# Moving one more block to transposed output, narrowing the key-value sums by two columns, and feeding the idle products from a constant

## The chip, the cores and the metric

The kernel runs on one core of one Trainium2 chip. The metric is device time in microseconds of that core for one execution; lower is better. Six executions of the kernel before lie within 0.7 us of each other (266.28 to 266.99). The granted TensorE clock was 1.0. The engines are called TensorE (PE in the profile; PEld is its weight load), DVE (vector), ScalarE (ACT), POOL and SP, which here only issues transfers.

## The reference, cut to what matters

```python
xn = layernorm(x)                                  # x: 2048 tokens x 640
q, k, v = split(xn @ wqkv)                         # 32 heads of 20
phi_q, phi_k = concat(softmax(+p), softmax(-p))    # p = q @ w_phi, k @ w_phi
kv = phi_k^T v ;  z = sum over tokens of phi_k     # per head, 40 x 20 and 40
o = (phi_q kv) / (phi_q z + 1e-6)
out = x + o @ wo + (silu(xn @ w1) * (xn @ w3)) @ w2     # hidden width 1536
```

Linear attention and a gated MLP share the normalised input. Their two output products are added to the residual `x`.

Of the kernel before, what the change touches and what calls it, by code (L numbers as in the profile page):

```python
# [3 lines left out]
ACT = mybir.ActivationFunctionType  # L4
ALU = mybir.AluOpType
# [4 lines left out]
D = 640  # L10
H = 32
# [234 lines left out]
def bass_parallel_sum__linear_kernel_hedgehog__glu_gated_swiglu__prompt_kernel(  # L246
# [14 lines left out]
    LEAD = 5  # L261
    AHEAD = 0
    PACE = 2.6
    f32 = DT.float32
    P = _Program(nc)

# [49 lines left out]
    WVK = new("WVK", [128, DC, 2 * D], bf, RKV)  # L316
    EqT0 = new("EqT0", [128, QC, 512], bf, RKV)
    xT2 = new("xT2", [128, DC, 512], bf, RKV)
    xT = {1: xT1, 2: xT2}

    RH = region(24576)
    hT0 = new("hT0", [128, FC, 512], bf, RH)
# [5 lines left out]
    w2_s = new("w2_s", [128, FC, D], bf, RE + 12288)  # L328
    EqT1 = new("EqT1", [128, QC, 512], bf, RE + 27648)
    hT = [hT0, hT1, hT2, hT3]  # L330
    ot = {1: new("ot1", [128, 4, D], bf, RH + 12288), 2: new("ot2", [128, 4, D], bf, RX)}

    RV = region(21504)
    v2 = new("v2", [128, T, H * 21], bf, RV)
    oT = new("oT", [128, DC, S], bf, RV)

    RW = region(13696)
# [57 lines left out]
    def memset(eng, o, v):  # L395
        P.op(eng, "memset", [o], [], (o, v), cost=0.15 + free(o) / 960)
# [52 lines left out]
    def consts_late():  # L449
        memset("POOL", FM[:], 1.0)  # L450
        select(FM[:], 0, [[0, 6], [-2 * DH, 3]], 1, ALU.is_ge, 0.0)
        select(FM[:], 2 * DH, [[0, 6], [2 * DH, 3]], -1, ALU.is_gt, 0.0)
        memset("POOL", v2[:].rearrange("p t (h c) -> p t h c", c=21)[:, :, :, DH], 1.0)


    def ln_sums(t, q):
# [39 lines left out]
    def ln_apply(t, lo=0, hi=D):  # L496
# [4 lines left out]
        else:  # L501
            P.op("ACT", "activation", [o], [o, s, z], (o, o, ACT.Identity), dict(bias=z, scale=s),
                 cost=0.9)

    def keep_warm(n, rep, rate=2400):
        for _ in range(rep):
            mm(bank(7, 128 * n), zero[:], zero[:].unsqueeze(1).to_broadcast([128, n, 128]), True, True,
               cost=128 * n / rate)

    def warm_up():  # L510
        keep_warm(4, 8, 1200)
        keep_warm(1, 9, 1200)

    def xn_transpose(t, k, c0=0, c1=DC):
        for dc in range(c0, c1):
# [30 lines left out]
        evac(dst.rearrange("p (b c) -> p b c", c=320), bank2(k, 320))  # L546


    def v_out(t, q, k):
        o = v2[:, t, 336 * q:336 * q + 336].rearrange("p (h c) -> p h c", c=21)[:, :, 0:DH]  # L550
        i = bank(k, 320).rearrange("p (h c) -> p h c", c=DH)
        if t < 2 or t == 2 and q == 0:
            copy("ACT", o, i)
        else:
            evac(o, i)

    def v_half(t, q, lo, hi):
        if lo == 0:
            held[t, q] = banks(1)
        k = held[t, q]  # L560
        for i in range(lo, hi):
            mm(bank(k, 320), xnT[:, i, t * 128:(t + 1) * 128], WVK[:, i, 320 * q:320 * q + 320],
               i == 0, i == DC - 1)
        if hi == DC:
            v_out(t, q, held.pop((t, q)))

    def v_first(lo, hi):
        if lo == 0:
            for q in range(2):
                held[0, q] = 2 + q  # L570
        for i in range(lo, hi):
            for q in range(2):
                mm(bank(2 + q, 320), xnT[:, i, 0:128], WVK[:, i, 320 * q:320 * q + 320], i == 0, i == DC - 1)
        if hi == DC:
            for q in range(2):
                v_out(0, q, held.pop((0, q)))
# [14 lines left out]
    def vk_features(t, k):  # L591
        for q, lo, hi in ((0, 0, 512), (1, 512, 1024), (2, 1024, 2 * D)):
            for i in range(DC):
                mm(bank(k + q, hi - lo), xnT[:, i, t * 128:(t + 1) * 128], WVK[:, i, lo:hi], i == 0, i == DC - 1)
        act(v2[:, t, :].rearrange("p (h c) -> p h c", c=21)[:, :, 0:DH],
            PS[:, 512 * k:512 * k + D].rearrange("p (h c) -> p h c", c=DH), ACT.Copy)
        k_exps(t, 512 * k + D)

    def q_features(t, k):
# [39 lines left out]
    def kv_sum(half, k):  # L639
        c0, c1 = ((0, 6), (6, QC))[half]  # L640
        for c in range(c0, c1):
            n = min(63, H * 21 - 63 * c)
            for t in range(T):
                m = min(128, (T - t) * 1280 - 120 * c)
                f = ekt[:].rearrange("p t f -> p (t f)")[:, 1280 * t + 120 * c:1280 * t + 120 * c + m]
                mm(bank(k, n, 63 * (c - c0))[0:m, :], f, v2[:, t, 63 * c:63 * c + n],
                   t == 0, t == T - 1, True, 0.03)
        w = c1 - c0 - half
        for a, b, g in ((0, w, 3), (w, c1 - c0, 2))[0:1 + half]:
            o = KVc[:, c0 + a:c0 + b, 0:21 * g].rearrange("p c (g d) -> p c g d", d=21)  # L650
            i = bank(k, 21 * g * (b - a), 63 * a).rearrange("p (c g d) -> p c g d", g=g, d=21)
            m = FM[:, a:b, 0:g]
            tt("DVE", o[:, :, :, 0:DH], i[:, :, :, 0:DH], m.unsqueeze(3).to_broadcast([128, b - a, g, DH]), ALU.mult)
            stt(o[:, :, :, DH], i[:, :, :, DH], DEN_EPS / 2, m, ALU.add, ALU.mult)

    def q_tok(t, k):
        b, j = divmod(t, 4)
# [78 lines left out]
        return min(range(0, 9 - n), key=free_at)  # L736

    done = dict.fromkeys(("w", "ln", "t", "f", "k", "v", "n", "kv", "p", "pn", "pt", "q", "o", "h", "m", "first", "t0"), 0)
    done.update({("u", b): 0 for b in range(NB)})

    landed, pace, force = {}, [0], [False]

# [51 lines left out]
    def k_norms():  # L794
        for t in range(T):
# [2 lines left out]
            yield lambda t=t: k_norm(t)  # L798
            done["n"] = t + 1

    def queries():
        while done["f"] < 3:
            yield None
        pace[0] = done["m"]
        for t in range(T):
            while done["pt"] < t - 2 or done["m"] < pace[0] + min(PACE, (NB * FC - 2 - pace[0]) / T) * (t - AHEAD):
                yield None
            while t >= 3 and landed[t - 3].end > P.free["PE"] + 1.3 and not force[0]:
                yield None
            yield lambda t=t: q_features(t, banks(2))  # L810
            done["p"] = t + 1
# [48 lines left out]
    def attention():  # L860
        yield warm_up
        for t in range(4):
            while done["t"] <= t:
                yield None
            if t == 0:
                for lo, hi in ((0, 2), (2, 4), (4, DC)):
                    while lo == 2 and done["t"] < 2:
                        yield None
                    yield lambda lo=lo, hi=hi: v_first(lo, hi)
                continue  # L870
            for q in range(2):
                for lo, hi in ((0, 3), (3, DC)):
                    yield lambda t=t, q=q, lo=lo, hi=hi: v_half(t, q, lo, hi)
        while done["f"] < 1:
            yield None
        for t in range(T):
            while done["t"] <= t:
                yield None
            if t < 4:
                yield lambda t=t: k_features(t, banks(2))  # L880
            else:
                yield lambda t=t: vk_features(t, banks(3))
            done["k"] = done["v"] = t + 1
            if 9 <= t < 14:
                while done["f"] < 2:
                    yield None
                yield lambda dc=t - 9: fold_mm(0, dc, banks(2))
        done["f"] = 3
        yield lambda: P.dma("SP", wo_s[:], A_wo.rearrange("(c p) d -> p c d", p=128))
        while done["n"] < T:  # L890
            yield None
        yield lambda: kv_sum(0, banks(1))
        yield lambda: kv_sum(1, banks(1))
        done["kv"] = 1
        yield lambda: P.dma("SP", w2_s[:], B_w2.rearrange("(c p) d -> p c d", p=128))
        yield lambda: (load_xres(0), load_xres(1))
        for t in range(T):
            while done["pt"] <= t or done["o"] < t - 2:
                yield None
            yield lambda t=t: q_tok(t, banks(2))  # L900
            done["q"] = t + 1
# [17 lines left out]
    def outs():  # L919
        for t in range(T):  # L920
            b = t // 4
            if b in xT:
                if t % 4 == 0:
                    while done["o"] < t + 4 or done["h"] <= b:
                        yield None
                    for dc in range(DC):
                        yield lambda b=b, dc=dc: out_chunk(b, dc, banks(1))
                        done["u", b] = dc + 1
                continue
            while done["o"] <= t or done["h"] <= b:  # L930
                yield None
            yield lambda t=t: out_tile(t, banks(2))
            done["u", b] = t % 4 + 1

    def turns():
        while done["u", 0] < 4:
            yield None
        yield lambda: load_xT(1)
        for b in xT:
            for dc in range(DC):  # L940
                while done["u", b] < DC:
                    yield None
                yield lambda b=b, dc=dc: turn_back(b, dc)
            if b == 1:
                yield lambda: P.dma("SP", xres[:], x_t[:, T - 4:T, :])
            yield lambda b=b: store(b)

    def late_loads():
        while done["q"] < 12:
            yield None  # L950
        yield lambda: load_xT(2)

    def set_held(d):
        held.clear()
# [92 lines left out]
```

## The kernel before: the parts that the change touches

The program is a list of "streams" (attention, queries, MLP units, outputs, transfers). A list scheduler inside the kernel file merges them into one fixed order per engine, by a cost model of its own. Tokens are handled in 16 tiles of 128, or 4 blocks of 512.

```python
def keep_warm(n, rep, rate=2400):                  # idle products, before any real work
    for _ in range(rep):
        mm(bank(7, 128 * n), zero[:], zero[:].unsqueeze(1).to_broadcast([128, n, 128]), ...)

def kv_sum(half, k):                               # kv and z: 11 chunks of 3 heads (the last has 2)
    for c in range(c0, c1):
        n = min(63, H * 21 - 63 * c)               # per head 20 values and a column of ones
        for t in range(T):                         # 11 x 16 = 176 products
            mm(bank(k, n, 63 * (c - c0))[0:m, :], f, v2[:, t, 63 * c:63 * c + n], ...)

def out_chunk(b, dc, k):                           # transposed output: 128 features x 512 tokens
    # 17 products of 512 columns, then DVE adds the transposed residual xT[b]
def turn_back(b, dc):                              # a transposing transfer back to token order
    P.dma("SP", ot[b][:, :, 128 * dc:128 * dc + 128], xT[b][:, dc, :], True)
def out_tile(t, k):                                # token order: 128 tokens x 640 features
    # 34 products of 320 columns, then DVE adds the residual xres
# xT = {1: xT1, 2: xT2}: blocks 1 and 2 use out_chunk, blocks 0 and 3 use out_tile
```

In `out_chunk` the weights are the stationary operand and the tokens stream, so each product has the full 512 columns. In `out_tile` the 640 features are cut into two products of 320.

The softmax here doesn't subtract the row's maximum and nothing guards it: scores larger than these inputs give would overflow.

## Time and profile before

| kernel before | |
|---|---|
| time, median of the runs taken beside the changed kernel | 266.47 us (266.28 to 266.99, 6 runs) |
| span of the profiled execution | 265.3 us |
| TensorE busy, DVE busy | 259.9 us (98%), 183.9 us (69%) |
| products (from the instruction order) | 1792, of which 18 idle |

The busy table, the chain of waits and the stretches by engine are shown inside the prediction below. First, the page's 40 equal slices of the span for DVE (a digit is the busy share in tenths):

```profile
DVE  4668999999796679696675858897979664221112
```

In the middle, where queries are handled, the digits are mixed, 5 to 9. Rows of TensorE's timeline (start, duration, engine, line, operation, count): the idle products, the key-value sums with what follows them, and the last products of the program.

```profile
1.05 3.97 PE L104 MATMUL PS<-zero 128*128 128x512 bf16 x17 [1.05 <-DVE warm L104]
...
81.37 5.27 PE L104 MATMUL PS<-v,ekt 128*128 128x63 bf16 x176
86.48 1.52 PE L104 MATMUL PS<-Wqp,xnT 128*128 128x360 bf16 x10
...
262.59 0.83 PE L104 MATMUL PS<-w_s,hT 128*128 128x128 bf16 x12
```

A duration holds the latency of the last product (5.27 us in the row of the sums, though the next row starts 5.11 us after it), so lengths are taken from start to start: the sums take 86.48 - 81.37 = 5.11 us. The stretch from the first product of the sums to the end of the last product, 262.59 + 0.83 - 81.37 = 182.05 us, is the best ruler of this study. It leaves out the front of the program, whose length varies from execution to execution (the first real product starts at 5.39 to 5.85 us in the traces). Below it is called **the ruler** and given to the nanosecond of the trace: 182.055 us.

### The profile page before, as it was taken

The numbers are of one execution on the slowest core, as the hardware profiler recorded it, in microseconds if no ns is written. First come the engines' busy times: TensorE is split into PE (matmuls) and PEld (weight loads), VectorE is DVE, ScalarE is ACT, GpSimd is POOL, SyncE is SP. The second block draws the span as 40 slices with busy tenths as digits, with TensorE's granted clock in tenths as the row PEclk, the third lists the DMA queues.
The fourth block names the chain that finished last, engine by engine and source line by source line (L and its number), as shares of the span: only waits on it lengthen the run. The fifth ranks groups of instructions, "written<-read, shape, count | busy, mean of one in ns | idle before, by whom it ended". The sixth has DMA issues, their size and how long they took to land.

```text
span 265.3 us, 4446 instructions
## 1 busy us (share of the span) xinstructions
PE 259.9 (98%) x1764; PEld 145.5 (55%) x1792; DVE 183.9 (69%) x316; ACT 106.2 (40%) x226; POOL 95.9 (36%) x107
## 2 busy tenths in 40 slices
PE   7999999999999999999999999999999999999997
PEld 3555545565558556466565745555554544444773
DVE  4668999999796679696675858897979664221112
ACT  5646988799870442251405224434540410000000
POOL 4311587989997035207030430442333020000000
DMA  6996068822300990921515078445751540463431
GB/s 220 284 315 176 4 160 237 174 52 52 121 2 16 260 214 20 158 52 53 107 25 104 2 133 150 57 79 102 123 94 25 101 79 0 93 127 125 104 126 49
DMA packets 72069, 29.03 MB, mean 109 GB/s; under 512 B 60272, under 2 KB 72048, under 8 KB 72048
## 3 DMA queue, kind: packets, MB, share of 16 engines
q1 hardware_dynamic: 71904, 28.58, 47.8%
q8 instruction: 14, 0.23, 0.4%
q10 hardware_dynamic: 144, 0.16, 0.2%
q14 instruction: 7, 0.06, 0.1%
HBM read 11.49 MB, written 2.62 MB: 53 GB/s over the span
## 4 chain that ended last, share of the span: by engine, by line
PE 96%; DVE 1%; DMA 1%; issue 1%; POOL 0%
PE PS L104 96%; DMA x_tok<-in_A_x_dram 1%; DVE bst L104 1%; DVE x_tok L104 0%; POOL rstd L104 0%; DVE mv L104 0%; DVE xres L104 0%; DVE xnT L104 0%
## 5 line engine op out<-in xcount | busy, mean ns | idle before, releaser
L104 PE MATMUL PS<-xnT,w_s 128*128 128x512 bf16 x463 | 105.6, 379 | 1.0 <-issue 0.2
L104 PEld LDWEIGHTS PS<-xnT,w_s 128*128 128x128 bf16 x480 | 46.2, 98 | 50.9 <-DVE xnT L104 0.3
L104 POOL TENSOR_TENSOR eqt<-eqt,rS 128x600 bf16<-128x600 bf16 (+1 forms) x32 | 41.1, 1306 | 91.1 <-DVE rS L104 91.1
L104 ACT ACTIVATE th<-PS 128x512 f32<-128x512 f32 x48 | 28.6, 595 | 68.0 <-PE PS L104 67.9
L104 DVE SCALAR_TENSOR_TENSOR t<-th,PS 128x512 bf16<-128x512 f32 x48 | 32.2, 672 | 25.3 <-ACT th L104 25.3
L104 PE MATMUL PS<-WVK,xnT 128*128 128x512 bf16 (+3 forms) x255 | 45.1, 329 | 0.3
L104 POOL TENSOR_TENSOR ekt<-ekt,rS 128x640 bf16<-128x640 bf16 x32 | 39.8, 1276 | 4.9 <-DVE rS L104 4.9
L104 ACT ACTIVATE eqt<-PS 128x240 bf16<-128x240 f32 (+1 forms) x96 | 27.2, 348 | 25.9 <-PE PS L104 24.1
L104 PEld LDWEIGHTS PS<-WVK,xnT 128*128 128x128 bf16 x260 | 24.1, 98 | 19.4 <-ACT WVK L104 0.4
L104 DVE SCALAR_TENSOR_TENSOR hT<-t,PS 128x512 bf16<-128x512 bf16 x48 | 33.0, 687 | 1.7
L104 PE MATMUL PS<-w_s,hT 128*128 128x320 bf16 (+2 forms) x192 | 27.5, 299 | 0.0
L104 PE MATMUL PS<-hT,w_s 128*128 128x512 bf16 x115 | 27.3, 379 | 0.3
L104 DVE TENSOR_REDUCE S<-ekt 128x64 f32<-128x1280 bf16 x16 | 23.3, 1455 | 2.2 <-ACT ekt L104 2.2
L104 DVE TENSOR_REDUCE S<-eqt 128x66 f32<-128x1320 bf16 x16 | 24.2, 1515 | 0.4 <-ACT eqt L104 0.4
L104 PE MATMUL PS<-Wqp,xnT 128*128 128x360 bf16 (+1 forms) x160 | 24.3, 299 | 0.0
L104 ACT ACTIVATE ekt<-PS 128x640 bf16<-128x640 f32 x32 | 22.3, 702 | 1.3 <-PE PS L104 0.8
L104 PEld LDWEIGHTS PS<-w_s,hT 128*128 128x128 bf16 x192 | 18.3, 98 | 7.8
L104 DVE TENSOR_TENSOR xT<-PS,xT 128x512 bf16<-128x512 f32 x10 | 6.9, 689 | 22.0 <-PE PS L104 22.0
L104 PEld LDWEIGHTS PS<-hT,w_s 128*128 128x128 bf16 x120 | 11.7, 98 | 14.2
L104 PEld LDWEIGHTS PS<-Wqp,xnT 128*128 128x128 bf16 x160 | 15.2, 98 | 7.6
L104 DVE RECIPROCAL rS<-S 128x64 f32<-128x64 f32 (+1 forms) x32 | 17.9, 560 | 1.1
L104 DVE TENSOR_TENSOR xres<-PS,xres 128x640 bf16<-128x640 f32 (+2 forms) x9 | 6.7, 744 | 17.1 <-PE PS L104 17.1
(55 smaller groups left out, 176.9 us busy)
## 6 DMA issues: line engine op xcount, KB each, us to landing
w_s<-in_B_w_dram SPq DMA_DIRECT2D x6, 640.0 KB, 6.4
x_tok<-in_A_x_dram SPq DMA_DIRECT2D x3, 640.0 KB, 5.2
w_s<-in_B_w_dram SPq DMA_DIRECT2D x1, 1920.0 KB, 8.9
out_dram<-ot SPq DMA_DIRECT2D x2, 640.0 KB, 4.7
out_dram<-xres SPq DMA_DIRECT2D x7, 160.0 KB, 1.9
wo_s<-in_A_wo_dram SPq DMA_DIRECT2D x1, 800.0 KB, 5.0
WVK<-in_A_wqkv_dram SPq DMA_DIRECT2D x2, 320.0 KB, 4.0
xres<-in_A_x_dram SPq DMA_DIRECT2D x4, 160.0 KB, 5.8
```

The source lines that it names most:

```text
L104: o = _Op(eng, lambda: m(*args, **kw), r, w, cost)
```

## The change

Its intent is to shave fixed costs off TensorE, which is always busy. Block 0 also gets the transposed output; the ones of the sums are shared by the heads of a chunk (61 columns in place of 63); the idle products read a constant that is there at the start. The queries are paced anew, since block 0's output no longer lies among them.

```diff
-    xT = {1: xT1, 2: xT2}
+    xT = {0: xT1, 1: xT1, 2: xT2}                  # blocks 0 and 1 share one buffer
-    v2 = new("v2", [128, T, H * 21], bf, RV)       # rows of 672 elements
+    v2 = new("v2", [128, T, QC * 61], bf, RV)      # rows of 671 elements
+    v2c = v2[:].rearrange("p t (c n) -> p t c n", n=61)
...
-            mm(bank(7, 128 * n), zero[:], zero[:].unsqueeze(1).to_broadcast([128, n, 128]), True, True,
+            mm(bank(7, 128 * n), one[:, 0:128], one[:, 0:128 * n], True, True, cost=128 * n / rate)   # one: the constant 1.0
-        keep_warm(1, 9, 1200)
+        keep_warm(1, 12, 1200)
...
+    VH = (0, 300, D)                               # value projection cut at 300, not 320
+        if q:
+            evac(v2c[:, t, 10, 1:41], bank(k, 40, 300))
...
-            n = min(63, H * 21 - 63 * c)
+            n = 61 if c < QC - 1 else 41
...
+    def paced(t):                                  # MLP units ahead of query tile t
+        left = NB * FC - 2 - pace[0]
+        return PACE0 * t if t < 4 else PACE0 * 4 + min(PACE, (left - PACE0 * 4) / 12) * (t - 4)
...
-        yield lambda: (load_xres(0), load_xres(1))
+        yield lambda: load_xT(0)
...
         for b in xT:                               # in turns(): transposes back, then the next load
+            if b == 0:
+                yield lambda: load_xT(1)
```

Cut: the evacuation of the sums, which now copies the one column of ones to three places, and the flags that order the loads.

More of the change, by code (lines that the diff above doesn't have):

```diff
@@ L263, in bass_parallel_sum__linear_kernel_hedgehog__glu_gated_swiglu__prompt_kernel @@
     PACE = 2.6
+    PACE0 = 2.6
     f32 = DT.float32
@@ L330, in bass_parallel_sum__linear_kernel_hedgehog__glu_gated_swiglu__prompt_kernel @@
     hT = [hT0, hT1, hT2, hT3]
-    ot = {1: new("ot1", [128, 4, D], bf, RH + 12288), 2: new("ot2", [128, 4, D], bf, RX)}
+    ot = {0: new("ot0", [128, 4, D], bf, RH), 1: new("ot1", [128, 4, D], bf, RH + 12288), 2: new("ot2", [128, 4, D], bf, RX)}
     RV = region(21504)
-    v2 = new("v2", [128, T, H * 21], bf, RV)
+    v2 = new("v2", [128, T, QC * 61], bf, RV)
+    v2c = v2[:].rearrange("p t (c n) -> p t c n", n=61)
     oT = new("oT", [128, DC, S], bf, RV)
@@ L452, in consts_late @@
         select(FM[:], 2 * DH, [[0, 6], [2 * DH, 3]], -1, ALU.is_gt, 0.0)
-        memset("POOL", v2[:].rearrange("p t (h c) -> p t h c", c=21)[:, :, :, DH], 1.0)
+        memset("POOL", v2c[:, :, :, 0], 1.0)
     def ln_sums(t, q):
@@ L503, in ln_apply @@
                  cost=0.9)
+    one = nc.const_aps.tensor(1.0, [128, 512], bf)
     def keep_warm(n, rep, rate=2400):
         for _ in range(rep):
-            mm(bank(7, 128 * n), zero[:], zero[:].unsqueeze(1).to_broadcast([128, n, 128]), True, True,
-               cost=128 * n / rate)
+            mm(bank(7, 128 * n), one[:, 0:128], one[:, 0:128 * n], True, True, cost=128 * n / rate)
     def warm_up():
         keep_warm(4, 8, 1200)
-        keep_warm(1, 9, 1200)
+        keep_warm(1, 12, 1200)
     def xn_transpose(t, k, c0=0, c1=DC):
@@ L546, in fold_mm @@
         evac(dst.rearrange("p (b c) -> p b c", c=320), bank2(k, 320))
+    VH = (0, 300, D)
     def v_out(t, q, k):
-        o = v2[:, t, 336 * q:336 * q + 336].rearrange("p (h c) -> p h c", c=21)[:, :, 0:DH]
-        i = bank(k, 320).rearrange("p (h c) -> p h c", c=DH)
+        o, i = v2c[:, t, 5 * q:5 * q + 5, 1:61], bank(k, 300).rearrange("p (c n) -> p c n", n=60)
         if t < 2 or t == 2 and q == 0:
@@ L561, in v_half @@
         for i in range(lo, hi):
-            mm(bank(k, 320), xnT[:, i, t * 128:(t + 1) * 128], WVK[:, i, 320 * q:320 * q + 320],
+            mm(bank(k, VH[q + 1] - VH[q]), xnT[:, i, t * 128:(t + 1) * 128], WVK[:, i, VH[q]:VH[q + 1]],
                i == 0, i == DC - 1)
@@ L572, in v_first @@
             for q in range(2):
-                mm(bank(2 + q, 320), xnT[:, i, 0:128], WVK[:, i, 320 * q:320 * q + 320], i == 0, i == DC - 1)
+                mm(bank(2 + q, VH[q + 1] - VH[q]), xnT[:, i, 0:128], WVK[:, i, VH[q]:VH[q + 1]],
+                   i == 0, i == DC - 1)
         if hi == DC:
@@ L594, in vk_features @@
                 mm(bank(k + q, hi - lo), xnT[:, i, t * 128:(t + 1) * 128], WVK[:, i, lo:hi], i == 0, i == DC - 1)
-        act(v2[:, t, :].rearrange("p (h c) -> p h c", c=21)[:, :, 0:DH],
-            PS[:, 512 * k:512 * k + D].rearrange("p (h c) -> p h c", c=DH), ACT.Copy)
+        act(v2c[:, t, :, 1:61], PS[:, 512 * k:512 * k + 660].rearrange("p (c n) -> p c n", n=60), ACT.Copy)
         k_exps(t, 512 * k + D)
@@ L645, in kv_sum @@
                 f = ekt[:].rearrange("p t f -> p (t f)")[:, 1280 * t + 120 * c:1280 * t + 120 * c + m]
-                mm(bank(k, n, 63 * (c - c0))[0:m, :], f, v2[:, t, 63 * c:63 * c + n],
-                   t == 0, t == T - 1, True, 0.03)
+                mm(bank(k, n, 61 * (c - c0))[0:m, :], f, v2[:, t, 61 * c:61 * c + n],
+                   t == 0, t == T - 1, True, 0.029)
         w = c1 - c0 - half
@@ L650, in kv_sum @@
             o = KVc[:, c0 + a:c0 + b, 0:21 * g].rearrange("p c (g d) -> p c g d", d=21)
-            i = bank(k, 21 * g * (b - a), 63 * a).rearrange("p (c g d) -> p c g d", g=g, d=21)
+            i = bank(k, 61 * (b - a - 1) + 1 + DH * g, 61 * a)
             m = FM[:, a:b, 0:g]
-            tt("DVE", o[:, :, :, 0:DH], i[:, :, :, 0:DH], m.unsqueeze(3).to_broadcast([128, b - a, g, DH]), ALU.mult)
-            stt(o[:, :, :, DH], i[:, :, :, DH], DEN_EPS / 2, m, ALU.add, ALU.mult)
+            if b - a > 1:
+                i = i.rearrange("p (c n) -> p c n", n=61)
+            else:
+                i = i.unsqueeze(1)
+            tt("DVE", o[:, :, :, 0:DH], i[:, :, 1:1 + DH * g].rearrange("p c (g d) -> p c g d", d=DH),
+               m.unsqueeze(3).to_broadcast([128, b - a, g, DH]), ALU.mult)
+            stt(o[:, :, :, DH], i[:, :, 0].unsqueeze(2).to_broadcast([128, b - a, g]), DEN_EPS / 2, m,
+                ALU.add, ALU.mult)
     def q_tok(t, k):
@@ L738, in bass_parallel_sum__linear_kernel_hedgehog__glu_gated_swiglu__prompt_kernel @@
     done = dict.fromkeys(("w", "ln", "t", "f", "k", "v", "n", "kv", "p", "pn", "pt", "q", "o", "h", "m", "first", "t0"), 0)
-    done.update({("u", b): 0 for b in range(NB)})
+    done.update({(k, b): 0 for k in "ux" for b in range(NB)})
     landed, pace, force = {}, [0], [False]
@@ L805, in queries @@
         for t in range(T):
-            while done["pt"] < t - 2 or done["m"] < pace[0] + min(PACE, (NB * FC - 2 - pace[0]) / T) * (t - AHEAD):
+            while done["pt"] < t - 2 or done["m"] < pace[0] + paced(t):
                 yield None
@@ L895, in attention @@
         yield lambda: P.dma("SP", w2_s[:], B_w2.rearrange("(c p) d -> p c d", p=128))
-        yield lambda: (load_xres(0), load_xres(1))
+        yield lambda: load_xT(0)
+        done["x", 0] = 1
         for t in range(T):
@@ L923, in outs @@
                 if t % 4 == 0:
-                    while done["o"] < t + 4 or done["h"] <= b:
+                    while done["o"] < t + 4 or done["h"] <= b or not done["x", b]:
                         yield None
@@ L929, in outs @@
                 continue
-            while done["o"] <= t or done["h"] <= b:
+            while done["o"] <= t or done["h"] <= b or not done["x", b]:
                 yield None
@@ L935, in turns @@
     def turns():
-        while done["u", 0] < 4:
-            yield None
-        yield lambda: load_xT(1)
         for b in xT:
@@ L943, in turns @@
                 yield lambda b=b, dc=dc: turn_back(b, dc)
+            if b == 0:
+                yield lambda: load_xT(1)
+                done["x", 1] = 1
             if b == 1:
                 yield lambda: P.dma("SP", xres[:], x_t[:, T - 4:T, :])
+                done["x", 3] = 1
             yield lambda b=b: store(b)
@@ L951, in late_loads @@
         yield lambda: load_xT(2)
+        done["x", 2] = 1
     def set_held(d):
```

## The prediction

> **What bounds the kernel now.** I read the busy table first, then the 40 slices, then the chain that ended last, then the TensorE timeline, then busy time by stretch.
>
> ```profile
> PE 259.9 (98%) x1764; PEld 145.5 (55%) x1792; DVE 183.9 (69%) x316; ACT 106.2 (40%) x226; POOL 95.9 (36%) x107
> ...
> PE PS L104 96%; DMA x_tok<-in_A_x_dram 1%; DVE bst L104 1%; DVE x_tok L104 0%; POOL rstd L104 0%; DVE mv L104 0%; DVE xres L104 0%; DVE xnT L104 0%
> ```
>
> TensorE is busy 98% of the 265.3 us span and 96% of the last chain is TensorE following itself. "Busy" alone could hide gaps, because the ends of matmuls are modelled. So I checked starts. These are timeline rows of TensorE (start, duration, what), from the end of the kernel:
>
> ```profile
> 237.45 1.24 PE L104 MATMUL PS<-oT,wo_s 128*128 128x512 bf16 x5
> ...
> 241.12 1.24 PE L104 MATMUL PS<-oT,wo_s 128*128 128x512 bf16 x5
> ...
> 244.79 1.52 PE L104 MATMUL PS<-wo_s,oT 128*128 128x320 bf16 x10
> 246.15 3.42 PE L104 MATMUL PS<-w_s,hT 128*128 128x320 bf16 x24
> 249.41 1.52 PE L104 MATMUL PS<-wo_s,oT 128*128 128x320 bf16 x10
> ```
>
> A transposed output chunk (17 products of 512 columns) takes 241.12 - 237.45 = 3.67 us, 215.9 ns each, where 512 columns at 2.4 GHz are 213.3. A token tile (34 products of 320) takes 249.41 - 244.79 = 4.62 us, 135.9 ns each against 133.3. Each product costs its columns plus about 2.5 ns, and nothing else.
>
> I then counted the whole program from the instruction order: 1792 products, 610,080 columns. Without the 18 idle products at the start (5,376 columns) that is 604,704 / 2400 = 252.0 us of columns plus 1774 x 2.5 ns = 4.4 us, 256.4 us in all. The first real product starts at 5.68 us and the last ends near 263.4, 257.8 us later. So all waiting of TensorE after its first product is about 1.4 us. Some 0.6 to 0.7 us of it lies before 7.09 us, where it waits for the layernorm of the first two tiles. Apparent gaps later (a dozen "0.05 issue" pieces) are single records missing from the trace: 1764 were recorded of 1792, and a start-to-start distance there is exactly one product longer. **The kernel is bound by the number of columns through TensorE**, and no stall of any size is left to remove.
>
> **What the Trainium skill says.** "TensorE: Matmul & The Clock Gate", section "Back-to-back issue gap", gives N/2.4 + 2.5 ns for a warm product with N columns. This trace agrees (215.9 and 135.9 ns above). The same page, "Wait — 56ns, not 53.3ns?", says that start to start never falls below about 25 ns. Here the key-value sums (176 products, 160 of 63 columns and 16 of 42) take 86.48 - 81.37 = 5.11 us, 29.0 ns each, near 63/2.4 + 2.5 = 28.8 and above that floor. The same page, "The HAM clock gate", says that the array starts at half rate and is released after about 3.4 us of activity. Here the idle products of 512 columns start 427 ns apart up to about 4.3 us, and the 128-column ones after them take 56 ns: the array is warm well before the first real product at 5.68.
>
> **The change part by part.** *Transposed output for block 0.* Removed: 4 token tiles, 136 products of 320. Added: 5 chunks, 85 products of 512. The columns are the same, 43,520. Time: 4 x 4.62 = 18.48 us against 5 x 3.67 = 18.35: **-0.13 us** on the path, only the fixed cost of 51 products. DVE: four adds of 0.82 us go, five of 0.69 come, +0.2 us, hidden. Transfers: two pairs of loads and four stores of 160 KB go. One transposing load (3.4 us of issue in the queue, 5.4 us to landing), five transposes back (1.3 us each) and one store of 640 KB come. All lie beside TensorE unless a chain forms (below).
>
> *Key-value sums of 61 columns.* 160 products lose 2 columns and 16 lose 1: 336 columns, 336 / 2400 = **-0.14 us** if they stay bound by columns, 0 if 29 ns is a floor of another kind. The values are now copied in groups of 60: projection splits of 300 and 340 instead of 320 and 320 (same columns and count, 0 us). The four early tiles get four extra copies of 40 columns, some 0.2 us each on ScalarE or DVE (the 40-column exponential takes 205 ns), beside other work. The one write of ones on POOL shrinks from 512 elements (2.37 us) to 176, hidden: TensorE enters the sums at 81.37 without a gap.
>
> *Idle products on a constant.* They no longer wait for DVE's zeros (1.05 us), so they may begin about 0.2 us earlier, and three more of 128 columns (3 x 56 ns) fill the end. They end before the first transpose can start (5.62 to 5.68 us, when layernorm is done). **0 us**, with less chance of a cold start.
>
> *Order.* The first four queries are now spaced 2.6 MLP units apart, and the first output chunk comes only after 16 more MLP units, 7 queries and 6 query products. The chunks 4 and 5 of block 0 move behind the last query. This moves work and adds none. The last instructions (five chunks of block 1, five of block 2, four token tiles) keep their order, so the tail of about 1.8 us after the last product stays.
>
> The sum: -0.13 - 0.14 = -0.27 us, 266.49 to 266.2 us.
>
> **The rivals.**
>
> *DVE becomes the bound in the first block.* Output tiles are TensorE time that asks little of DVE (4.62 us against 0.82), and they leave just the stretch with queries. From the end of the key-value sums to the first chunk, the new order has 16 MLP units, 7 query projections and 6 query products. TensorE: 16 x 2.16 + 7 x 1.36 + 6 x 0.32 = 46 us. DVE: 16 x (0.67 + 0.69) + 7 x (1.52 + 0.57) + 6 x (0.25 + 0.53 + 0.24 + 0.45) = 21.8 + 14.6 + 8.8 = 45.2 us, 98%. Before, the corresponding work with three tiles in it ran at 78% in the row for 88 to 138 below:
>
> ```profile
> core 0: us, PE busy (x) PEld busy (x) DVE busy (x) ACT busy (x) POOL busy (x), PEclk, DMA share, GB/s
> ...
> 26.00:50.00 24.00, 23.84 (x134) 12.39 (x136) 23.26 (x42) 19.99 (x30) 17.32 (x21) 1.00 0.62 154
> 50.00:74.00 24.00, 23.84 (x154) 13.71 (x155) 21.40 (x29) 20.59 (x32) 22.53 (x23) 1.00 0.28 69
> ...
> 88.00:138.00 50.00, 49.67 (x340) 29.09 (x344) 38.85 (x66) 17.21 (x48) 14.01 (x12) 1.00 0.51 113
> 138.00:175.00 37.00, 36.78 (x240) 20.63 (x242) 27.56 (x44) 14.01 (x37) 11.63 (x9) 1.00 0.47 84
> 175.00:222.00 47.00, 46.68 (x276) 23.56 (x280) 36.15 (x62) 14.62 (x41) 12.84 (x10) 1.00 0.45 82
> 222.00:265.30 43.30, 41.27 (x249) 23.05 (x250) 9.61 (x16) 0.00 (x0) 0.00 (x0) 1.00 0.38 96
> ```
>
> The columns are the stretch, its length, then busy time and count by engine. Against this rival: from 26 to 50 us DVE was busy 23.26 of 24 us, 97%, and TensorE did not stall. A DVE that keeps 97% would need 45.2 / 0.97 = 46.6 us for 46 us of TensorE. The eight accumulator banks absorb a lag of several us (three MLP units of two banks are 6.5 us). I expect 0 to 0.5 us of stall, at worst some 2 us: up to 268.
>
> *A chain of transfers behind block 0.* Blocks 0 and 1 share one buffer for the residual. Block 1's adds must wait for block 0's last add (0.7), five transposes (6.9 of issue, 2.5 to land) and the new load (5.4): about 15.5 us after block 0's last chunk. TensorE makes four chunks of 3.67 us meanwhile and holds four of eight banks; it would stall only beyond about seven chunks, 25 us. The residual load for the last block then follows block 1's transposes; I work it out to land some 8 us before the first tile's add. Hidden, unless transfers take twice as long. Then it would cost 2 to 5 us.
>
> *The front gets better or worse.* The waits before 7.09 us are for layernorm, which the change does not touch. The extra copies could delay an evacuation of the transposes by 0.1 to 0.3 us; an earlier warm clock could win 0.1.
>
> **The range and the chances.** I add 0.1 us of expected stall to 266.2 and predict 266.3 us. Low 265.8: both savings, and 0.4 us from the front and the noise between runs (266.28 to 266.64 before). High 267.3: no savings from the sums and about 1 us of DVE stalls. Faster by over 2% would mean below 261.2 us, under the 256.4 - 0.27 us of products plus the 5.68 before and some 3 us after them (1.8 of tail, 1.2 between span and time), so near zero: 0.01. Slower by over 2% means over 5.3 us of stall, which only the transfer chain together with DVE could make: 0.02. Within 2%: 0.97.
>
> **What would show each step right or wrong.** Output chunks of block 0 at 3.67 us each, 85 products. Key-value sums in about 4.97 us instead of 5.11 (wrong if still 5.1). Idle products starting near 0.85 us and the first transpose still near 5.68. DVE near 95 to 98% busy in the 46 us after the sums, with TensorE gaps there of at most 0.5 us in all; a larger gap ended by DVE or ScalarE evacuating an accumulator would be the first rival. Around 208 to 228 us the first add of block 1 should wait for the residual load for about 12 us while TensorE has no gap; a gap there would be the second. The prediction is wrong if the span between the first and last product is over 258.5 or under 257.0 us.

## The result, and the profile after

The changed kernel takes 266.26 us (266.12 to 266.32, 6 runs), against 266.47 us for the kernel before in the same rounds. The ratio is 0.9989, with a 95% interval of 0.9976 to 1.0002: the same within 2%, and 0.2 us less by the medians. A ratio is the mean time of one kernel's fast runs over that of the other's fast runs of the same rounds, so it is not quite the ratio of the medians.

The page after: the busy table's row, DVE's slices and the summary of the chain of waits.

```profile
PE 260.4 (98%) x1716; PEld 141.0 (53%) x1744; DVE 183.0 (69%) x319; ACT 106.9 (40%) x228; POOL 94.4 (36%) x107
...
DVE  4668999999796679989995979897986103221112
...
PE PS L104 95%; DMA x_tok<-in_A_x_dram 1%; DVE t L104 1%; DVE hT L104 0%; DVE bst L104 0%; POOL rstd L104 0%; DVE mv L104 0%; DVE x_tok L104 0%; DVE xres L104 0%
```

TensorE is as full as before. DVE's work is the same in sum but sits earlier: the 17th to 22nd digit (106 to 146 us) read 989995 where they read 696675, and the 31st to 34th (199 to 225 us) read 6103 where they read 9764. DVE's MLP operations now have 1% of the chain. TensorE's timeline after, the same places as before:

```profile
0.84 4.62 PE L104 MATMUL PS<-const-bfloat16-1.0 128*128 128x512 bf16 x20 [0.84 <-PEq L1051]
...
81.40 5.16 PE L104 MATMUL PS<-v,ekt 128*128 128x61 bf16 x176
86.41 1.52 PE L104 MATMUL PS<-Wqp,xnT 128*128 128x360 bf16 x10
...
200.56 1.24 PE L104 MATMUL PS<-oT,wo_s 128*128 128x512 bf16 x5
...
204.22 1.24 PE L104 MATMUL PS<-oT,wo_s 128*128 128x512 bf16 x4
...
262.39 0.83 PE L104 MATMUL PS<-w_s,hT 128*128 128x128 bf16 x12
```

The sums take 5.01 us, 0.10 less. A chunk of block 0, the fourth, takes 204.22 - 200.56 = 3.66 us, as foretold. The ruler is 181.822 us, 0.233 less than before. The front gave back 0.03 us (81.40 against 81.37). Nothing else moved: the start-to-start distances on TensorE after 12 us that are clearly longer than their product are single missing records, but for one of 0.1 us near 26 us, as in the trace before.

DVE in the stretch that worried the prediction (columns as in the prediction: stretch, length, then busy time and count of PE, PEld, DVE, ACT, POOL):

```profile
86.41:132.35 45.94, 45.62 (x297) 24.37 (x300) 40.00 (x72) 19.82 (x53) 15.41 (x12) 1.00 0.60 123
86.41:100.00 13.59, 13.49 (x84) 7.04 (x83) 9.38 (x22) 6.22 (x17) 2.57 (x2) 1.00 1.01 233
```

DVE was busy 40.0 of 45.9 us, 87%, not 98%. It is idle at first (69% up to 100 us, waiting for the first MLP unit after the sums), so from 100 to 132.35 us it was busy 30.62 of 32.35 us, 95%, and a few us of its share were still to be done when the stretch ended. TensorE did not stall.

The transfers behind block 0, from SP's timeline (when a transfer was issued), then DVE's adds with what they waited for:

```profile
206.36 6.42 SPq L116 DMA_TRANSPOSE ot<-xT  x5
214.04 2.87 SPq L116 DMA_TRANSPOSE xT<-in_A_x_dram  x1
```

```profile
208.09 0.69 DVE L104 TENSOR_TENSOR xT<-PS,xT 128x512 bf16<-128x512 f32 x1 [2.98 <-PE PS L104]
219.08 1.89 DVE L104 TENSOR_TENSOR xT<-PS,xT 128x512 bf16<-128x512 f32 x3 [10.30 <-PE PS L104]
```

The add at 208.09 is that of block 0's last chunk, whose products end at 207.9 us. The transposes back of the earlier chunks were already being issued by then. Block 1's residual was issued at 214.04 into the shared buffer, and at 219.08 three adds of block 1 run together, after 10.3 us in which DVE had nothing to do. The bracket names TensorE, whose third chunk of block 1 ended at that moment; but the first of these three chunks had been ready since 211.6, so what held its add was the load, which lands some 5 us after its issue. TensorE went on meanwhile without a gap.

### The profile page after: what moved, and what is told of

The parts are those of the page before. It is cut to its first block, busy times and chain, and to the rows that moved or that the text cites. A ratio compares the mean times of both kernels' runs of the same rounds, so it can differ in the third digit from the quotient of the medians.

```text
span 265.1 us, 4353 instructions
## 1 busy us (share of the span) xinstructions
PE 260.4 (98%) x1716; PEld 141.0 (53%) x1744; DVE 183.0 (69%) x319; ACT 106.9 (40%) x228; POOL 94.4 (36%) x107
## 4 chain that ended last, share of the span: by engine, by line
PE 95%; DVE 2%; DMA 1%; issue 1%; POOL 0%
PE PS L104 95%; DMA x_tok<-in_A_x_dram 1%; DVE t L104 1%; DVE hT L104 0%; DVE bst L104 0%; POOL rstd L104 0%; DVE mv L104 0%; DVE x_tok L104 0%; DVE xres L104 0%
## 5 line engine op out<-in xcount | busy, mean ns | idle before, releaser
L104 PE MATMUL PS<-WVK,xnT 128*128 128x512 bf16 (+4 forms) x255 | 45.1, 329 | 0.3
L104 PE MATMUL PS<-hT,w_s 128*128 128x512 bf16 x179 | 41.1, 379 | 0.0
L104 ACT ACTIVATE eqt<-PS 128x240 bf16<-128x240 f32 (+1 forms) x96 | 27.2, 348 | 27.7 <-PE PS L104 25.9
L104 DVE TENSOR_TENSOR xT<-PS,xT 128x512 bf16<-128x512 f32 x15 | 10.1, 685 | 34.7 <-PE PS L104 31.6
L104 PEld LDWEIGHTS PS<-hT,w_s 128*128 128x128 bf16 x180 | 17.6, 98 | 21.3
L104 PE MATMUL PS<-oT,wo_s 128*128 128x512 bf16 x70 | 17.9, 379 | 0.3
L104 DVE TENSOR_TENSOR o_tok<-PS,g_s 128x360 bf16<-128x360 f32 (+1 forms) x32 | 15.7, 491 | 1.1
L104 DVE BATCH_NORM_STATS2 bst<-x_tok 128x6 f32<-128x320 bf16 x30 | 13.9, 481 | 2.8 <-DMA x_tok<-in_A_x_dram 2.4
```

What stands on the lines that cost most here:

```text
L104: o = _Op(eng, lambda: m(*args, **kw), r, w, cost)
```

## The experiments

Eleven more kernels ran, all correct. The ruler (first product of the key-value sums to the end of the last product) of the six that add no work, beside the two kernels; each ruler is read from one trace:

| kernel | ruler, us | against before | key-value sums, us | time: median (range), runs |
|---|---|---|---|---|
| before | 182.055 | | 5.113 | 266.47 (266.28 to 266.99), 6 |
| sums alone (e1) | 181.951 | -0.104 | 5.009 | 266.40 (266.14 to 266.50), 5 |
| idle products alone (e2) | 182.056 | +0.001 | 5.114 | 266.39 (266.13 to 266.47), 5 |
| block 0 and pacing alone (e3) | 181.930 | -0.125 | 5.116 | 266.51 (266.15 to 267.34), 6 |
| changed | 181.822 | -0.233 | 5.009 | 266.26 (266.12 to 266.32), 6 |
| changed, old pacing (e4) | 181.824 | -0.231 | 5.009 | 266.24 (265.97 to 268.12), 6 |
| changed, padded rows, old idle products (g1) | 181.790 | -0.265 | 4.975 | 266.60 (265.94 to 268.19), 6 |
| changed, padded rows (g3) | 181.787 | -0.268 | 4.973 | 266.15 (266.07 to 266.49), 5 |

### Each part alone (e1, e2, e3)

Edit of e1: the lines of the diff on `v2`, `VH` and the sums, in the kernel before. Edit of e2: only `keep_warm` and `warm_up`. Edit of e3: only `xT`, the loads, the order of outputs and `paced`.

> The kernel before with one part of the change: value groups of 60 columns, key-value sums of 61 and 41 columns, splits of 300 and 340. Theory (bound by columns): the 176 products of the sums take about 5.0 us instead of 5.11, the stretch from TensorE's first real product to its last shrinks by 0.10 to 0.14 us, the time goes from 266.5 to about 266.35 us. Rival (29 ns is a floor set by something else, such as the weight loads): the sums stay at 5.1 us and the time at 266.5. The extra copies of 40 columns cost TensorE nothing after 12 us in either theory; before 12 us at most 0.1 us.

> The kernel before with only the idle products on the constant, three more of them. Theory: they start near 0.84 instead of 1.05 us and change nothing behind the first real product; 266.5 us, within 0.1. Rival: products of ones, or their earlier start, move the moment at which the array clock is released (4.0 us in the trace of before, 5.05 in that of after), and a later release makes real products slow or costs up to 0.3 us.

> The kernel before with only the transposed output of block 0 and the spread queries. Theory: 85 products of 512 columns for 136 of 320 save 51 fixed costs of 2.5 ns, 0.13 us in the stretch from first to last real product; 266.35 us, no TensorE gap. Rival (DVE or the transfer chain gives it back): gaps on TensorE between 86 and 135 us or between 204 and 245 us, and a time of 266.5 or more.

TensorE's timeline of e1:

```profile
81.26 5.16 PE L104 MATMUL PS<-v,ekt 128*128 128x61 bf16 x176
86.27 1.52 PE L104 MATMUL PS<-Wqp,xnT 128*128 128x360 bf16 x10
```

The same places in e3, and its end:

```profile
81.14 5.27 PE L104 MATMUL PS<-v,ekt 128*128 128x63 bf16 x176
...
262.23 0.83 PE L104 MATMUL PS<-w_s,hT 128*128 128x128 bf16 x12
```

The parts add up: -0.104 + 0.001 - 0.125 = -0.228 us, and the whole change is -0.233. The sums gain 0.104, so 29 ns was no floor, but less than the 0.14 of the prediction. Block 0 gains 0.125 of the expected 0.13. The idle products, which start at 0.84 us as expected, change nothing from the sums on. What they might do to the front lies outside the ruler; there only the times speak, with 0.5 us less to 0.1 us more for e2 (0.9981 to 1.0005).

The times, in contrast, cannot tell these kernels apart: their ratios to the kernel before are 0.9994, 0.9993 and 1.0002, each with an interval of about 0.0012 to either side. The front is the reason for most of it. The first product of the sums starts anywhere from 81.14 to 81.50 us in these traces, and that scatter is larger than either gain. Some runs also have 1.2 us more between span and time than the rest (the run of 267.34 us in e3 has a span of 264.9), which is outside the kernel. Two single runs, 268.12 in e4 (clock 0.998) and 268.19 in g1, have a span of 266.9 all the same; no trace of them was kept, and their cause stays open. They and two runs of the other kind lift g1's ratio to 1.0023 (1.0000 to 1.0047), though g1's trace (of a run of 266.09) shows nothing slower.

### The pacing (e4)

Edit: the changed kernel without `paced`, with the old condition.

> The changed kernel without the spreading of the first four queries (the old pacing). Theory (TensorE is never short of work in either order): same products, same 266.3 us as the changed kernel, within 0.1. Rival (the spread is what keeps DVE from stalling TensorE): TensorE gaps between 86 and 140 us of 0.5 us or more in all and a time of 266.8 or more.

The ruler is 181.824 us, 0.002 from the changed kernel, with no gap on TensorE. The spread queries are worth nothing in time.

### How much room DVE has (f1, f2, g2)

Edit, in each kernel, with zero net weight in the scheduler's cost model so that the order of every engine stays (the traces confirm it). f1 and f2 also carry the probes of the idle products that their expectations describe; these end before the ruler begins.

```diff
     def q_norm(t):
+        P.op("DVE", "tensor_reduce", [junk[:, 0:66]], [ev], ..., cost=0.08)   # the sum once more, unused
         normalise(ev, QC, 6)
```

> The kernel before, with DVE's sum over each query tile made twice (16 more reductions of 1.51 us, 24 us in all, the result of the extra one unused; the order on every engine is kept). If DVE's room in the kernel before is as wide as its 76% busy between 86 and 222 us says, it goes to about 94% there and TensorE loses under 1.5 us: 266.5 to 268 us. Besides, the idle products read ones written by DVE instead of zeros, with the same pattern and the same start: if the data decide when the array clock is released, the release moves from 4.2-4.5 us to 4.9 us or later; if not, it stays.

> The changed kernel with the same 16 extra reductions. Its queries and MLP units lie closer together (output chunks of block 0 moved behind them), so theory: DVE would need 126 us in the 118 us between 86 and 204, and TensorE is made to wait 5 to 10 us: 271 to 276 us. Rival (the spread gives DVE as much room as before): no more than the kernel before loses with them. Besides, the idle products read the constant but begin only behind DVE's first writes (near 1.05 us): if the start decides, the release of the clock moves back to 4.2-4.5 us; if the data or the repeated single element decide, it stays at 4.9 us or later.

> The changed kernel without the spread of the first four queries, with the 16 extra reductions on DVE that cost the kernel before 4.8 us and the changed kernel 12.7. If the spread is what buys DVE room once the output of block 0 is gone from among the queries, this one loses more than 12.7 us: 280 us or more. If it buys none, 279 us or less.

By the ruler, the kernel before lost 186.907 - 182.055 = 4.85 us, the changed one 194.610 - 181.822 = 12.79 us, and the changed one with the old pacing 190.947 - 181.824 = 9.12 us. Each ran once, so its state is unknown; f1's granted clock was 1.0. The stretch from 88 to 138 us in f1, then in f2:

```profile
88.00:138.00 50.00, 47.95 (x324) 27.27 (x328) 43.58 (x66) 16.88 (x48) 12.86 (x10) 1.00 0.48 112
```

```profile
88.00:138.00 50.00, 44.46 (x278) 22.85 (x282) 45.73 (x69) 18.68 (x52) 15.41 (x12) 1.00 0.52 103
```

In f2 DVE is busy 45.7 of 50 us and TensorE only 44.5: the roles are changed. In f2 the waits have DVE's name on them, as in the first of these rows of TensorE's timeline. In f1 most of the waiting ends with a transfer, the transpose of a query's features, as in the second:

```profile
105.99 1.24 PE L104 MATMUL PS<-xnT,w_s 128*128 128x512 bf16 x5 [1.95 <-DVE t L104]
```

```profile
131.71 0.48 PE L104 MATMUL PS<-KVc,EqT 128*128 128x63 bf16 x11 [0.80 <-DMA EqT<-eqt]
```

Summed by what ended them, TensorE's waits after the sums are 10.9 of 11.6 us by DVE itself in f2, and in f1 1.9 of 4.8 us by DVE and 2.9 by such transposes. The chain that ended last in f1 leads from that transfer back to DVE (126.84 us, an output add), behind which it was issued.

What follows: the change did spend room on DVE. Under this load it loses some 8 us more than the kernel before (6 without the slow clock named below), though none of that shows in the time. My expectation for f1 (under 1.5 us) was a miss, and so was that for f2 (5 to 10 us; it lost 12.8). An average of 76% over 136 us hid stretches without room (in f1 DVE is busy 32.1 of the 34 us from 100 to 134), and work that is merely late on DVE starts its transfers late. And g2 went the way of "it buys none": the old pacing loses less than the new, so the spread queries are not what protects TensorE from DVE. The numbers hold a share that isn't DVE's: in f2 (from 206.84 us) and in g2 (from 110.40 us) the clock record shows half rate for 3.4 us after such waits, about 1.7 us of each loss. Without it the order stays: 4.9, 11.1 and 7.4 us.

### How much room the transfers have (f3, f4)

Edit: the five transposes back of block 0 issued again, three more times (f3) or once more (f4), ahead of the load into the shared buffer. The same kernels carry the front and width probes described in their expectations.

```diff
+            for _ in range(3 * (b == 0)):          # f4: range(1 * ...)
+                for dc in range(DC):
+                    yield lambda b=b, dc=dc: turn_again(b, dc)
             if b == 0:
                 yield lambda: load_xT(1)
```

> The changed kernel with the five transposes back of block 0 issued four times over (15 more, same data), which delays the load of block 1's residual into the shared buffer by about 19 us, from landing at 219 to landing near 238. Theory (eight banks of accumulator are the slack): TensorE runs on until the ninth chunk at about 233.5 us finds no free bank, waits some 5 us there, and the end moves by 5 to 8 us. Rival (the chain has more slack than worked out): no gap. Besides, there are no idle products before the first real ones: if they are worth anything, the real products up to about 9 us run at half rate and the first MLP unit begins 0.5 to 1.5 us later.

> The changed kernel with 11 x 16 extra products ahead of the key-value sums, 41, 45, ... 81 columns wide, each with its own weights as in the sums, results unused: the start-to-start time per width. Theory of the prediction: N/2.4 + 2.5 ns, so 27.9 at 61, 28.7 at 63, 36.3 at 81 ns, and a floor of 25 ns below 54 columns. Rival: the slope is softer near the floor, which would be why two columns were worth 0.6 and not 0.83 ns. They add about 5.2 us. Besides, the transposes back of block 0 are issued twice over (five more): the load of block 1's residual lands about 6.5 us later, near 225.5, and TensorE shows no gap (eight banks hold). Also the idle products read zeros through the constant's pattern (one element repeated), started by DVE near 1.05 us: release near 4.2-4.5 us if data or start decide, later if the pattern does.

With one more round (f4) TensorE shows no gap. With three (f3), DVE's first add of block 1 starts at 240.98 us, and TensorE's timeline reads:

```profile
241.73 2.32 PE L104 MATMUL PS<-oT,wo_s 128*128 128x512 bf16 x5 [3.31 <-DVE xT L104]
243.84 3.33 PE L104 MATMUL PS<-hT,w_s 128*128 128x512 bf16 x12
247.01 1.24 PE L104 MATMUL PS<-oT,wo_s 128*128 128x512 bf16 x5
```

Eight chunks ran ahead without their adds, and the ninth waited 3.31 us for a bank. After that the five products take 243.84 - 241.73 = 2.11 us instead of 1.08: the clock had fallen to half, and stayed there for 3.4 us, another 1.7 us. So the chain is real, and eight banks are what gives it room. The load into the shared buffer was issued 6.5 us later than in the changed kernel in f4 and 21 us later in f3 (fronts taken out); f3's wait of 3.3 us puts the room at about 17 us. The end of the last product came 6.1 us later than in the changed kernel: 1.23 from the front, 3.3 of wait and 1.6 of slow clock.

The 1.23 us are the worth of the idle products, to within the front's scatter of about 0.4 us: without them the sums start at 82.63 us instead of 81.40. The clock record of f3 shows half rate until 9.48 us.

The width probe of f4, mean start-to-start time of 16 products of each width (61 columns: also the sums themselves), from the starts in the trace:

| columns | 41 | 45 | 49 | 53 | 57 | 61 | 65 | 69 | 73 | 77 | 81 |
|---|---|---|---|---|---|---|---|---|---|---|---|
| ns | 25.4 | 25.3 | 25.2 | 25.5 | 27.2 | 28.7 | 30.6 | 32.2 | 34.1 | 35.5 | 37.4 |

There is a floor of 25.2 to 25.5 ns up to 53 columns. From 57 to 81 the slope is (37.4 - 27.2) / 24 = 0.43 ns per column, about one column at 2.4 GHz, so 61 and 63 columns lie on the sloping part. The rival of a soft slope falls: two columns ought to be worth 0.85 ns. The level is 0.8 to 1.2 ns above N/2.4 + 2.5. The probe also shows what TensorE's being the bound means: it made the sums and itself last 10.246 us instead of 5.009, and the ruler grew from 181.822 to 187.059, by the same 5.237 us.

### The missing 0.035 us (g1, g3)

Edit of g3: one element of padding per row of values, nothing else. g1 also has the idle products of the kernel before.

```diff
-    v2 = new("v2", [128, T, QC * 61], bf, RV)
-    v2c = v2[:].rearrange("p t (c n) -> p t c n", n=61)
+    v2 = new("v2", [128, T, QC * 61 + 1], bf, RV)
+    v2c = v2[:, :, 0:QC * 61].rearrange("p t (c n) -> p t c n", n=61)
```

> The changed kernel with two edits: each row of the values padded from 671 to 672 elements, and the idle products as the kernel before has them (zeros written by DVE, 9 narrow ones). The sums are 0.104 us shorter in all three traces with 61 columns than in all three with 63 (5.009 against 5.113 to 5.116), where 2 columns should give 0.14. If the odd row length costs some products a few ns, the padded sums take 4.90 to 4.95 us; if not, 5.01. The stretch from the second tile's transposes to the last product is 256.10 us in the changed kernel: 256.0 or 256.1 here. The array clock is released at 4.2 to 4.5 us again (5.05 in the changed kernel). Time 266.1 to 266.3 us, which the runs cannot tell from 266.26.

> The changed kernel with one edit: each row of the values padded from 671 to 672 elements. With the padding (and other idle products) the sums took 4.975 us, 0.034 less than unpadded and 0.138 less than with 63 columns in rows of 672, as 336 columns at 2.4 GHz would (0.140). If the row length is the cause, the sums take 4.975 us here too and the stretch from the second tile's transposes to the last product is 256.06 us against 256.10 in the changed kernel; if it was chance, 5.009 and 256.10. The time stays at 266.1 to 266.3 us, the difference of 0.03 being below what runs show.

The sums take 4.975 and 4.973 us with rows of 672 elements, and 5.009 in all three plain traces with rows of 671. The expected 4.90 to 4.95 was too bold. Between rows of equal length, 63 to 61 columns is worth 5.113 - 4.973 = 0.140 us. That this is just 336 / 2400 is in part luck: the 16 products of 42 or 41 columns lie on the floor and gained nothing (25.9 ns each before, 26.1 in g3), so all of it comes from the other 160, at 0.44 ns per column. One element less per row gave 0.035 us back.

The starts in the traces show more of how: a product's time goes with where its values begin. With rows of 671 elements the beginning moves by two bytes from one token tile to the next, and over seven traces the products of 61 columns take 31.3 ns where they begin 14 bytes after a multiple of 16 (counted from the start of the buffer), 29.7 at 8 bytes, and 27.8 to 28.7 at the other six. With rows of 672 the beginning is fixed within a chunk: 14 bytes give 29.3 ns against 28.2 to 28.9 in g1 and g3, and 30.1 against 29.0 to 29.4 in the sums of 63 columns. No run moved the beginning alone, so that it is the cause, and not only goes along, is not shown.

The stretch from the second tile's transposes, named in the expectations, is no good for g3: that tile came early (6.81 us) and TensorE then waited at the front, so it reads 256.48 us. The ruler, which starts behind the front, is 181.787 us.

g3 is the shortest version by the ruler, 0.035 us below the changed kernel. Its time, 266.15 us at a ratio of 0.9990 to the kernel before (0.9976 to 1.0003), cannot be told from 266.26.

### When the array clock is released (a theory that fell)

After the first traces I thought that the constant (one element repeated) delays the release of the clock: with the tile of zeros it came at 4.1 to 4.5 us in three traces, with the constant at 4.9 us or later in three. f1 (ones in the tile of zeros: 4.09) ruled out the data, f2 (the constant, started late: 5.45) the start. But then g1 released at 5.78 us with zeros, and g3 at 3.63 us and g2 at 4.58 us with the constant. Both kinds cover the same range. What sets the moment stays open; the runs show only that it varies by over 2 us from execution to execution.

## Why the prediction was right

- **The bound.** Right. TensorE's products set the time: the parts add up to within 0.005 us, and added products lengthen the ruler one for one (f4). The first real product starts at 5.77 us and the last ends at 263.22, 257.45 us later, within the 257.0 to 258.5 named.
- **Block 0, -0.13 us.** Right: -0.125 (e3).
- **Sums, -0.14 us.** The mechanism was right and the size was off: -0.104 (e1). The term that was mis-sized is "336 columns, 336 / 2400". It left out that rows of values became 671 elements long, which cost 0.035 us; with 672 the term is 0.140 (g3). It also counted 16 columns of the narrowest chunk, which lie on the floor and are worth nothing. The reading behind it, "29.0 ns each, near 28.8", was an average over both widths: the products of 63 columns took 29.4 ns, 0.6 above the formula, and those of 42 took 25.9.
- **Splits and extra copies, 0 us.** Right after 12 us: the way from there to the first product of the sums is the same within 2 ns in e1 and in e3, which keeps the old splits. Before 12 us the front's own scatter (the sums start at 81.14 to 81.50 us) hides anything smaller.
- **Idle products, 0 us.** Right as far as can be seen: +0.001 after the front (e2), and no difference in the times. "With less chance of a cold start" was not borne out: the release came anywhere from 3.6 to 6.3 us, with either kind.
- **DVE as the bound.** The stall of 0 to 0.5 us was right (none), but the load was over-counted: 98% was foretold for the 46 us and 87% measured, because work due at the end of a stretch spills over it and DVE idles at its start. That DVE's room shrinks was right, and f1 and f2 show by how much.
- **The chain of transfers.** Right that it is hidden, and that the eight banks are its slack (f3, f4). Its length was over-counted: 15.5 us after block 0's last chunk foretold, 219.08 - 207.9 = 11.2 us measured, because the transposes of the first four chunks did not wait for the fifth.
- **The sum.** -0.27 foretold, -0.233 by the ruler, -0.21 by the medians. 266.3 foretold, 266.26 measured. The 0.1 us added for stalls did not occur and made up for the sums' shortfall and the front's 0.03, so part of the closeness of the total is luck.

## What to carry to other kernels

When one engine is busy without gaps, price a change by that engine's instructions alone: their count times the fixed cost, their columns times the column time, and nothing for what moves elsewhere. To measure gains below the scatter of whole runs, take a stretch of the trace that begins behind the noisy front; there 0.1 us was repeatable to a few nanoseconds (sums of 61 columns in plain rows 5.005 to 5.012 us in seven traces, of 63 columns 5.113 to 5.116 in four) where medians of six runs were not. And a change that costs nothing now can still spend another engine's room: load that engine on purpose, in both versions with the order kept, to see what is left.

## What the Trainium skill lacked or had wrong

- "TensorE: Matmul & The Clock Gate", "Back-to-back issue gap": its table gives about 60 cycles (25 ns) for 1 to 64 columns. Here the floor ends between 53 and 57 columns: 25.5 ns at 53, 27.2 at 57, 28.7 at 61. The section also calls the prediction's N/2.4 + 2.5 the gap of an isolated product, and gives 131 ns at 512 columns for a stream with a weight load per product; the streams here, with a load per product, took 215.9 ns.
- No page has it with a time for TensorE ("SBUF — State Buffer" tells of lines of 16 bytes and of a penalty for crossing them): where the streamed operand begins matters for narrow products. At 61 columns, 14 bytes after a multiple of 16 took 31.3 ns, most other places about 28; rows of 671 elements against 672 cost 0.035 us over 176 products (5.009 against 4.973 us).
- "TensorE: Matmul & The Clock Gate", "HAM oscillation", which warns of idle gaps over some 3.4 us: in f2 the clock fell to half for 3.4 us from 206.84 us after TensorE had been busy 2.00 of the 3.80 us before, with no single gap over 1.7 us. In g2 it fell at 110.40 us, 1.25 us after a gap of 2.97 us. The page's next section, "A second HAM failure mode: psum-queue depth-cycling", does tell of short idles that do this, but gives no length for them.
- Same page, "What you observe", which gives about 4 us with 500 ns of scatter for the release of the cold clock: here it came 2.8 us after the first idle product at the earliest (g3, 3.63 against 0.84) and more than 5 us after it at the latest (f4, about 6.3 against 1.05).
